# Attention on 64-row halves and half of a dense network moved behind it: an attention and expert kernel on one core

## Chip, core and metric

One NeuronCore of a Trainium2 chip runs the whole program. The metric is the device time of one execution, in microseconds; the time before is the median of three runs, 517.41 us (515.21 to 519.56). PE is the matrix engine (PEld its weight loads), DVE the vector engine, ACT the scalar engine with the activation functions, POOL the general engine that also issues the software DMA queue, SP the engine that only issues DMAs.

## The reference

```python
q_n, k_n = rmsnorm(q, g_q), rmsnorm(k, g_k)          # batch 8, 12 heads, 448 tokens, 64 wide
scores = q_n @ k_n.T / sqrt(64)
attn = exp(scores - max) ; attn /= attn.sum(-1) + 1e-9
x = (attn @ v).transpose(0, 2, 1, 3).reshape(3584, 768)
y_dense = relu(x @ w1_dense) @ w2_dense              # 768 -> 512 -> 768
expert = argmax(x @ w_gate) ; gate = its softmax weight  # 8 experts
out = y_dense + gate * (relu(x @ w1[expert]) @ w2[expert])
```

All arrays are float32; `rmsnorm(x, g)` is x divided by the root of its mean square over the 64 elements, times g. Each token goes to one expert.

## The kernel before

**Attention.** Work runs over 48 head pairs t (8 batches of 6). Two pairs share one load: q and k come as float32 through SP, v as bf16 through POOL. A head's 448 tokens lie on 112 partitions, 4 tokens each (L141, pieces of 1024 bytes). POOL squares q and k (L161), DVE sums them (L162), ACT makes the reciprocal root by Ln and Exp (L167, L168), DVE normalises both (L177). PE transposes them (L186), DVE copies the result out of PSUM, multiplying q by both gains (L191, L193). For each quarter j of the keys PE makes the scores of both heads, each on its 64 rows of the array (L202), and ACT one Exp over both, 896 elements a partition (L204). PE multiplies the exponentials with v and a column of ones (L215, four key quarters into each of four query blocks); DVE divides by that column (L219, L221). The attention output of a pair is transposed (L228) and copied by ACT (L230). After six pairs `route` makes the logits, picks the expert, and writes the bf16 rows and the gate weight to a table of records in DRAM (L260 to L264).

**Dense network.** Both dense GEMMs of the batch before (`dense1`, L273, and `dense2`, L284) are cut into pieces and laid between the attention steps. The float32 result goes into the records as well (L293). A record is 1536 bytes of x, 3072 of dense result, 256 with the gate.

**Order.** The order on PE, POOL and SP is the written one; a scheduler orders DVE and ACT. For each t the loop puts the scores of t+1, the transposes of t+2, the values of t and the dense pieces in turn; loads are issued one group (two pairs) ahead of their squares. The 16 expert weights (float32 in DRAM, cast to bf16 in flight on POOL's queue, 768 KB each in the chip) are issued every 2.5 pairs (L329).

**Slot plan and slot tiles.** After attention DVE ranks all tokens by expert at once (L360 to L442): counts by scans, one selection matrix of 128x4096 (L410), a matrix of slots (L413, L416), and 32 matmuls that put the token numbers in slot order (L422). Then 35 tiles of 128 slots follow: POOL gathers their records (L449, four tiles ahead), PE transposes x (L460), multiplies with the expert's first matrix, chosen by a register (L469), ACT applies relu and gate (L474), PE transposes (L479) and multiplies with the second (L487), DVE adds the dense result (L493), and POOL scatters the rows to the output (L495).

Of the kernel before, what the change touches and what calls it, by code (L numbers as in the profile page):

```python
# [8 lines left out]
F32 = mybir.dt.float32  # L9
BF16 = mybir.dt.bfloat16  # L10
# [7 lines left out]
def kernel(  # L18
# [21 lines left out]
    JJ = 4  # L40
    SC = S // JJ
# [4 lines left out]
    FT = F // P  # L46
    De = D + 1
    scale = 1.0 / (D ** 0.5)
    QC = (0, 128, 256, S - 128)
# [6 lines left out]
    nc.vector.memset(eps_t, 1e-6)  # L56
    gq2 = const.tile([P, 1], F32)
    gk2 = const.tile([P, 1], F32)
    for hh in range(2):
        nc.sync.dma_start(gq2[hh * D:(hh + 1) * D, :], g_q.unsqueeze(1))  # L60
        nc.sync.dma_start(gk2[hh * D:(hh + 1) * D, :], g_k.unsqueeze(1))
# [4 lines left out]
    EB = E * KD * F  # L66
    NTL = N // P + E - 1
    XH = Dm // 2
    GO = XH + Dm
    NC4 = 4 * B  # L70
    tri = const.tile([P, P], BF16)
    ones = const.tile([P, P], BF16)
    nc.vector.memset(ones, 1.0)
    nc.gpsimd.affine_select(tri, ones, pattern=[[1, P]], compare_op=ALU.is_gt, fill=0.0,
                            base=0, channel_multiplier=-1)
    iop = const.tile([P, P], BF16)
    nc.gpsimd.iota(iop, pattern=[[1, P]], base=0, channel_multiplier=0,
                   allow_small_or_imprecise_dtypes=True)
    iot = const.tile([P, NTL], F32)
    nc.gpsimd.iota(iot, pattern=[[1, NTL]], base=0, channel_multiplier=0,  # L80
                   allow_small_or_imprecise_dtypes=True)
    iom = const.tile([P, NTL], F32)
    nc.vector.tensor_scalar(iom, iot, float(P), None, op0=ALU.mult)
    prio = const.tile([P, E], F32)
    nc.gpsimd.iota(prio, pattern=[[-1, E]], base=E, channel_multiplier=0,
                   allow_small_or_imprecise_dtypes=True)
    col = const.tile([P, 4], F32)
    for mi in range(4):
        nc.gpsimd.iota(col[:, mi:mi + 1], pattern=[[0, 1]], base=QC[mi], channel_multiplier=1,
                       allow_small_or_imprecise_dtypes=True)  # L90
    cmp3 = const.tile([P, 4, JJ - 1], F32)
    for jj in range(1, JJ):
        nc.vector.tensor_scalar(cmp3[:, :, jj - 1], col, float(jj * SC), None, op0=ALU.is_ge)
    colj = const.tile([P, 4], F32)
    nc.vector.tensor_reduce(colj, cmp3, AX.X, ALU.add)
    colp = const.tile([P, 4], F32)
    nc.vector.scalar_tensor_tensor(colp, in0=colj, scalar=-float(SC), in1=col,
                                   op0=ALU.mult, op1=ALU.add)
    tok = const.tile([P, B, 4, 3], BF16)
    for b in range(B):  # L100
        nc.vector.memset(tok[:, b, :, 0], float(b + 1))
        nc.vector.tensor_copy(tok[:, b, :, 1], colj)
        nc.vector.tensor_copy(tok[:, b, :, 2], colp)
    nc.vector.memset(tok[:D, :, 3, :], 0.0)

    RC = Dm // 2 + Dm + 64
    rec = nc.dram_tensor("records", (N, RC), F32).ap()
    oh = const.tile([P, B, 4, E], BF16)
    wgb = const.tile([P, KD, E], BF16)
    wd1 = const.tile([P, KD, F], BF16)  # L110
    wd2 = const.tile([P, FT, Dm], BF16)
    we = const.tile([P, E, 2, KD * F], BF16)

# [9 lines left out]
    with tc.tile_pool(name="a_ld", bufs=3) as ld, \  # L123
         tc.tile_pool(name="a_sb", bufs=2) as sb, \
         tc.tile_pool(name="a_sc", bufs=2, space=bass.MemoryType.PSUM) as scp, \
         tc.tile_pool(name="a_wk", bufs=4, space=bass.MemoryType.PSUM) as wkp:
        gts = [sb.tile([P, 4, RC - GO], F32, name=f'gt{i}', tag=f'gt{i}', bufs=1) for i in range(2)]
        for gt in gts:
            nc.vector.memset(gt, 0.0)
        xin, ssqs, rs, xn, qkT, exs, vas, xnats, xTs, hTs, vrs = [{} for _ in range(11)]  # L130

        def load(g):
            if g * GP >= NT:
                return
            b, h0 = divmod(g * GP * 2, H)
            parts = ((0, 2), (2, 4)) if g == 0 else ((0, 2 * GP),)
            for name, src in (("q", q), ("k", k)):
                xin[name, g] = ld.tile([SC, 2 * GP, JJ * D], F32, tag="x" + name, name="x" + name)
            for a, z in parts:
                for name, src in (("q", q), ("k", k)):  # L140
                    nc.sync.dma_start(  # L141
                        xin[name, g][:, a:z],
                        src[b, h0 + a:h0 + z].rearrange("h (p j) d -> p h (j d)", j=JJ))
            vr = ld.tile([SC, 2 * GP, JJ * D], BF16, tag="vr")
            nc.gpsimd.dma_start(vr, v[b, h0:h0 + 2 * GP].rearrange("h (p j) d -> p h (j d)", j=JJ))
            vrs[g] = vr
            ssqs[g] = sb.tile([SC, 2, 2 * GP * JJ], F32, tag="ssq", name="ssq")

        def values(g):
            va = ld.tile([SC, 2 * GP, JJ, D + 2], BF16, tag="va")  # L150
            nc.vector.memset(va[:, :, :, D:], 1.0)
            nc.vector.tensor_copy(va[:, :, :, :D], vrs[g].rearrange("p h (j d) -> p h j d", d=D))
            vas[g] = va

        def squares(t, names="qk"):
            g, i = divmod(t, GP)
            for name in names:
                n = "qk".index(name)
# [37 lines left out]
        def scores(t, j):  # L196
            if j == 0:
                exs[t] = sb.tile([SC, JJ, 2, S], BF16, tag="ex", name="ex")
# [353 lines left out]
```

## Time and profile before

| | us |
|---|---|
| median of the runs | 517.41 |
| the profiled execution | 519.15 |
| its span from first to last instruction | 517.3 |
| PE busy | 399.3 |
| DVE busy | 326.6 |
| ACT busy | 274.8 |
| POOL busy | 205.3 |
| first exp | 28.1 |
| last matmul of the last routing ends | 337.7 |
| first gather | 373.9 |
| first expert matmul | 383.1 |

The busy times overlap: engines work side by side, so that shares of the span add up to more than one. What counts in a stage is the engine or transfer whose end the next step waits for. The DMA engines were busy for 73% of the span (45.4% for POOL's queue, 27.6% for SP's). PE's clock was granted at 0.92 of full speed on average.

### The profile page before, as it was taken

Reading aid. Unit: us, or ns where it says so; the run is one execution under the profiler, and the core shown is the slowest. Engines: PE = TensorE matmul, PEld = TensorE weight load, DVE = VectorE, ACT = ScalarE, POOL = GpSimd, SP = SyncE. Lnnn points to the kernel's source line nnn. Section 1 sums busy time; section 2 is a strip of 40 time slices with the busy share of each in tenths; the row PEclk is TensorE's granted clock in tenths of the full one; section 3 lists DMA queues with packets and bytes.
Section 4 is the critical chain, followed back from the end, with each engine's and each line's share of the span. In section 5 each row is a group of like instructions: output and inputs, shape, how many; then the busy total and the mean of one; then the engine's idle time right before and its main releaser. Section 6 shows DMA issues by size and latency. Waiting matters only on the chain.

```text
span 517.3 us, 10774 instructions
## 1 busy us (share of the span) xinstructions
PE 399.3 (77%) x4010; PEld 232.7 (45%) x4010; DVE 326.6 (63%) x761; ACT 274.8 (53%) x431; POOL 205.3 (40%) x223
## 2 busy tenths in 40 slices
PE   0189888769688887788977979980249889899894
PEld 0046645435344454454543545650215555556552
DVE  3796999868568779588786975427603434444442
ACT  0077887648567756767855978730003333333331
POOL 6674354453426327128136130000023555556542
PEclk9999999979888989979977999996559999999998
DMA  8999679997798599959879441251063878888860
GB/s 142 237 218 175 151 154 159 192 256 96 176 269 137 137 271 142 198 133 239 187 134 248 107 144 30 81 152 46 1 241 122 278 253 266 286 283 266 294 259 2
DMA packets 66017, 92.62 MB, mean 179 GB/s; under 512 B 8749, under 2 KB 56109, under 8 KB 65968
## 3 DMA queue, kind: packets, MB, share of 16 engines
q0 software_dynamic: 31568, 52.48, 45.4%
q1 hardware_dynamic: 34400, 39.46, 27.6%
q8 instruction: 33, 0.54, 0.4%
q14 instruction: 16, 0.13, 0.1%
HBM read 83.16 MB, written 31.20 MB: 221 GB/s over the span
## 4 chain that ended last, share of the span: by engine, by line
PE 30%; DMA 27%; DVE 20%; ACT 7%; issue 6%; POOL 6%; SPq 2%; POOLq 0%; DVEq 0%; ACTq 0%
DMA xq<-in_q_dram 9%; DMA xg<-records,row 9%; DMA xk<-in_k_dram 8%; DVE y L177 7%; PE he L469 5%; PE av L215 5%; DVE ssq L162 5%; PE ps L202 5%; PE yp L487 4%; ACT ex L204 4%; POOL sq L161 4%; PE ff L273 4%; PE ff L284 2%; DVE xa L221 2%; PE tr L186 2%
## 5 line engine op out<-in xcount | busy, mean ns | idle before, releaser
L204 ACT ACTIVATE ex<-ps 112x896 bf16<-112x896 f32 x192 | 173.8, 921 | 54.3 <-PE ps L202 52.7
L161 POOL TENSOR_TENSOR sq<-xq 112x512 f32<-112x512 f32 x48 | 52.1, 1085 | 141.8 <-DMA xq<-in_q_dram 118.8
L162 DVE TENSOR_REDUCE ssq<-sq 112x8 f32<-112x512 f32 x96 | 64.0, 672 | 42.9 <-POOL sq L161 42.9
L202 PE MATMUL ps<-y 64*112 64x448 bf16 x384 | 84.1, 435 | 2.5 <-DVE y L193 1.3
L215 PE MATMUL av<-va,ex 112*128 112x65 bf16 x1536 | 71.2, 202 | 17.7 <-DVE xa L221 16.0
L215 PEld LDWEIGHTS <-ex 112*128 112x128 bf16 x1536 | 59.3, 103 | 40.9 <-DVE xa L221 21.3
L284 PE MATMUL ff<-wd,hT 128*112 128x384 bf16 x256 | 60.4, 347 | 10.8 <-DVE xa L221 10.8
L449 POOL DMA_INDIRECT xg<-records,row x35 | 33.9, 967 | 81.1 <-DVE dest L442 70.4
L186 PE MATMUL tr<-ident,y 112*128 112x112 bf16 x384 | 39.2, 232 | 29.0 <-DVE y L177 24.2
L161 POOL TENSOR_TENSOR sq<-xk 112x512 f32<-112x512 f32 x48 | 51.3, 1070 | 19.1 <-DVE ssq L162 9.8
L495 POOL DMA_INDIRECT out_dram<-ys,dest x35 | 35.6, 1018 | 58.6 <-DVE ys L493 58.6
L474 ACT ACTIVATE hs<-he,xg 128x512 bf16<-128x512 f32 x35 | 24.0, 687 | 65.6 <-DMA xg<-records,row 36.3
L469 PE MATMUL he<-we,xT 128*128 x210 | 53.5, 393 | 3.0 <-issue 1.5
L462 DVE COPY xT<-xp 128x768 bf16<-128x768 bf16 x35 | 19.5, 557 | 57.5 <-PE xp L460 57.5
L202 PEld LDWEIGHTS <-y 64*112 64x112 bf16 x384 | 26.2, 131 | 61.6 <-issue 56.0
L273 PE MATMUL ff<-xT,wd 128*128 128x448 bf16 x192 | 52.1, 373 | 2.1 <-DVE xa L221 2.1
L487 PE MATMUL yp<-we,heT 128*128 x280 | 51.2, 326 | 0.8 <-DVE ys L493 0.8
L493 DVE TENSOR_TENSOR ys<-yp,xg 128x768 f32<-128x768 f32 x35 | 33.5, 957 | 28.0 <-PE yp L487 28.0
L481 ACT COPY heT<-hp 128x512 bf16<-128x512 bf16 x35 | 20.5, 586 | 49.1 <-PE hp L479 49.1
L186 PEld LDWEIGHTS <-y 112*128 112x128 bf16 x384 | 22.9, 104 | 51.0 <-DVE y L177 25.3
L177 DVE TENSOR_TENSOR y<-xq,r 112x512 bf16<-112x512 f32 x48 | 45.0, 937 | 0.9 <-ACT r L168 0.9
L221 DVE TENSOR_TENSOR xa<-av,inv 128x256 bf16<-128x256 f32 x96 | 40.1, 418 | 1.4
(98 smaller groups left out, 473.3 us busy)
## 6 DMA issues: line engine op xcount, KB each, us to landing
we<-in_moe_w_dram POOLq DMA_DIRECT2D x16, 768.0 KB, 8.4
records<-ys SPq DMA_DIRECT2D x32, 336.0 KB, 3.3
xq<-in_q_dram SPq DMA_DIRECT2D x23, 448.0 KB, 6.7
xk<-in_k_dram SPq DMA_DIRECT2D x23, 448.0 KB, 7.0
vr<-in_v_dram POOLq DMA_DIRECT2D x24, 224.0 KB, 5.9
records<-xa SPq DMA_DIRECT2D x8, 576.0 KB, 7.4
wd<-in_moe_w_dense_dram POOLq DMA_DIRECT2D x2, 768.0 KB, 19.4
records<-xa SPq DMA_DIRECT2D x8, 96.0 KB, 7.0
```

The source lines that it names most:

```text
L161: nc.gpsimd.tensor_mul(sq, x, x)
L162: nc.vector.tensor_reduce(ssqs[g][:, n, 2 * i * JJ:(2 * i + 2) * JJ], sq.rearrange("p h (j d) -> p (h j) d", d=D), AX.X, ALU.add)
L177: nc.vector.tensor_mul(y.rearrange("p j h d -> p h j d"), x.rearrange("p h (j d) -> p h j d", d=D), rs[g][:, n, 2 * i * JJ:(2 * i + 2) * J ...
L186: nc.tensor.transpose(ps[:, j * SC:(j + 1) * SC], xn[name, t][:, j].rearrange("p h d -> p (h d)"), ident[:SC, :SC])
L202: nc.tensor.matmul(ps[:, hh, :S], qkT["k", t][d0:d0 + D, j * SC:(j + 1) * SC], qkT["q", t][d0:d0 + D, :], start=True, stop=True)
L204: nc.scalar.activation(exs[t][:, j], ps[:, :, :S], AF.Exp, scale=scale)
L215: nc.tensor.matmul(av[:, mi], exs[t][:, j, hh, QC[mi]:QC[mi] + P], vas[t // GP][:, 2 * (t % GP) + hh, j, :De], start=(j == 0), stop=(j == ...
L221: nc.vector.tensor_mul(xnats[b][:, :, h * D:(h + 1) * D], av[:, :, :D], inv.to_broadcast([P, 4, D]))
L273: nc.tensor.matmul(ffs[0], wd1[:, kk, ff * P:(ff + 1) * P], xTs[b][:, kk], start=(kk == 0), stop=(kk == KD - 1))
L284: nc.tensor.matmul(ffs[0], hTs[b][:, ff, j * SC:(j + 1) * SC], wd2[:, ff, dd * Dm // 2:(dd + 1) * Dm // 2], start=(ff == 0), stop=(ff == F ...
L469: nc.tensor.matmul(he, xTs[t][:, kk], we[:, bass.ds(eregs[t], 1), 0, kk * F:(kk + 1) * F] .rearrange("p o f -> p (o f)"), start=(kk == 0), ...
L487: nc.tensor.matmul(yp[:, dd, :HD], heTs[t][:, ff], we[:, bass.ds(eregs[t], 1), 1, ff * Dm + dd * HD:ff * Dm + (dd + 1) * HD] .rearrange("p ...
```

## The change

**Layout.** A head's 448 tokens lie on 64 partitions, 7 tokens each; two heads are stacked on the two partition halves, and a group is four heads (two such stacks), so 24 groups take the place of 48 pairs. Every operation outside PE then works on 128 partitions and 896 elements. Scores are made for 64 keys at a time and run on four 64x64 tiles of the array; values take 64 rows each.

**Norm of k.** k is loaded as bf16 through POOL's queue and never normalised. Its reciprocal root, with the factor 1/8 inside, becomes the per-partition scale of the Exp, which now covers one head (448 elements) at a time.

**Dense.** Only the first dense GEMM stays in attention; it is made token by token row, so that relu(x w1) goes into the record as 512 bf16 values. A record is 1536 bytes of x, 1024 of this, 256 with the gate. The second dense GEMM is made in the slot tiles, into the same PSUM sums as the expert's second matrix.

**Slot plan.** `route` ranks the tokens of its batch at once, with running counts, and makes its part of the selection matrix. Each expert has at least one tile.

**Weights.** Exponentials live in the space of the last experts' weights, so the last eight weight loads (experts 4 to 7) are issued among the first eight slot tiles, and the others every 2.6 groups.

The core of the diff (`...` marks what is left out):

```diff
-        nc.sync.dma_start(gq2[hh * D:(hh + 1) * D, :], g_q.unsqueeze(1))
-        nc.sync.dma_start(gk2[hh * D:(hh + 1) * D, :], g_k.unsqueeze(1))
+        nc.scalar.dma_start(gq2[hh * D:(hh + 1) * D, :], g_q.unsqueeze(1))
+        nc.scalar.dma_start(gk2[hh * D:(hh + 1) * D, :], g_k.unsqueeze(1))
...
-    GO = XH + Dm
+    GO = XH + F // 2
+    RC = GO + 64
+    LATE, WPACE = 8, 2.6
...
-         tc.tile_pool(name="a_sc", bufs=2, space=bass.MemoryType.PSUM) as scp, \
+         tc.tile_pool(name="a_sc", bufs=4, space=bass.MemoryType.PSUM) as scp, \
          tc.tile_pool(name="a_wk", bufs=4, space=bass.MemoryType.PSUM) as wkp:
+        NX = 2 * J
+        xflat = we.rearrange("p e a f -> p (e a f)")[:, -NX * 2 * S:]
...
+            return src.rearrange("b h s d -> (b h) s d")[h0:h0 + n].rearrange(
+                "(i r) (p j) d -> (r p) i (j d)", r=2, j=J)
+                xin["q", g] = ld.tile([P, 2, J * D], F32, tag="xq", name="xq", bufs=3)
+                nc.sync.dma_start(xin["q", g], heads(q, 4 * g, 4))
+                for name, src in (("k", k), ("v", v)):
+                    nc.gpsimd.dma_start(xs[name][:, n[0]:n[1]],
+                                        heads(src, 8 * u + 2 * n[0], 2 * (n[1] - n[0])))
...
+            nc.scalar.activation(r, r, AF.Exp, scale=-0.5,
+                                 bias=lns_t if name == "k" else 0.0)
...
+            for j in ((0, 1, 2, 3), (4, 5, 6))[part]:
+                for hh in range(2):
+                    nc.tensor.transpose(ps[hh * D:(hh + 1) * D, j], x[:, hh, j * D:(j + 1) * D],
+                                        ident)
...
+            pss = [scp.tile([P, 512], F32, tag="sc", name="sc") for hh in range(2)]
             for hh in range(2):
-                d0 = hh * D
-                nc.tensor.matmul(ps[:, hh, :S], qkT["k", t][d0:d0 + D, j * SC:(j + 1) * SC],
-                                 qkT["q", t][d0:d0 + D, :], start=True, stop=True)
-            nc.scalar.activation(exs[t][:, j], ps[:, :, :S], AF.Exp, scale=scale)
+                rows = slice(hh * D, (hh + 1) * D)
+                for r in range(GP):
+                    nc.tensor.matmul(pss[hh][r * D:(r + 1) * D, :S], kT[rows, r, j],
+                                     qT[rows, r].rearrange("p j s -> p (j s)"),
+                                     start=True, stop=True)
+            for hh in range(2):
+                nc.scalar.activation(x[:, hh], pss[hh][:, :S], AF.Exp,
+                                     scale=rs["k", g][:, hh, j:j + 1])
...
+            if m == 0:
+                for r in range(GP):
+                    avs[r] = wkp.tile([P, 4, De], F32, tag="wk", name="av")
+            for j in range(J):
+                for r in range(GP):
+                    rows = slice(r * D, (r + 1) * D)
+                    nc.tensor.matmul(avs[r][:, m], exs[g, j][rows, hh, QC[m]:QC[m] + P],
+                                     va[rows, hh, j, :De], start=(j == 0), stop=(j == J - 1))
...
-            nc.scalar.copy(xTs[b][:, pr], ps)
+            nc.vector.tensor_copy(xTs[b][:, gb * GP:(gb + 1) * GP], ps)
...
             nc.vector.tensor_tensor(oh[:, b], hot, m2.to_broadcast([P, 4, E]), ALU.is_equal)
+            nc.vector.memset(oh[:D, b, 3, :], 0.0)
+            rk = wkp.tile([P, 5, E], F32, tag="wk", name="rk")
+            mm = [(rk[:, :4], tri, oh[:, b])]
+            mm += [(rk[:, i:4], ones, oh[:, b, :4 - i]) for i in range(1, 4)]
+            mm += [(rk[:, 4:], ones, oh[:, b, m:m + 1]) for m in range(4)]
...
+            nc.vector.tensor_tensor(sel[:, b], iop.unsqueeze(1).to_broadcast([P, 4, P]),
+                                    lo[:, b].unsqueeze(2).to_broadcast([P, 4, P]), ALU.is_equal)
...
+        def dense(b, m, part):
+            if part == 0:
+                ff[0] = wkp.tile([P, F], F32, tag="wk", name="ff")
+            for kk in range(2 * part, 2 * part + 2):
+                nc.tensor.matmul(ff[0], xTs[b][:, kk, QC[m]:QC[m] + P], wd1[:, kk],
+                                 start=(kk == 0), stop=(kk == KD - 1))
+            if part == 2:
+                hd = sb.tile([P, F], BF16, tag="hd", bufs=1)
+                nc.scalar.activation(hd, ff[0], AF.Relu)
+                nc.sync.dma_start(rec[r0:r0 + n, XH:GO], hd[P - n:].bitcast(F32))
...
+                for g in range(NG + 1):
+                    if g % 2 == 0:
+                        load_kv(g // 2 + 2)
+                    load_q(g + 5)
+                    while nw < len(wjobs) - LATE and (nw - 2) * WPACE <= g + 1:
+                        nc.gpsimd.dma_start(*wjobs[nw])
+                    for i in range(J):
+                            scores(g + 1, i)
+                        if g + 2 < NG and i in (1, 2, 4, 5):
+                            transposes(g + 2, "qk"[i // 3], (i - 1) % 3)
+                            for n in ((0,), (1,), (2, 3), (4,), (5,), (6,), (7,))[i]:
+                                attend(g, n // 4, n % 4)
...
+            hp = ps1.tile([P, FT, P], BF16, tag="tr")
+            for i in range(FT):
+                nc.tensor.transpose(hp[:, i], xb[:, Dm + i * P:Dm + (i + 1) * P], ident)
+            nc.vector.tensor_copy(hdTs[t], hp)
...
-            eregs[t] = nc.tensor.value_load(tei[:, t:t + 1], min_val=0, max_val=E - 1)
+            eregs[t] = nc.tensor.value_load(tei[:, t:t + 1], min_val=0, max_val=min(t, E - 1))
...
+                    nc.tensor.matmul(yp[:, dd, :HD], hdTs[t][:, i],
+                                     wd2[:, i, dd * HD:(dd + 1) * HD],
+                                     start=(i == 0), stop=False)
...
-            nc.vector.tensor_add(ys, yp[:, :, :HD],
-                                 xgs[t][:, XH:GO].rearrange("p (a d) -> p a d", a=2))
+            nc.vector.tensor_copy(ys[:, 0], yp[:, 0, :HD])
+            nc.scalar.copy(ys[:, 1], yp[:, 1, :HD])
...
+                if len(wjobs) - LATE + t < len(wjobs):
+                    nc.gpsimd.dma_start(*wjobs[len(wjobs) - LATE + t])
```

## The prediction

> **What bounds the kernel now.** I read the busy time of each engine stage by stage first, then the timeline of two undisturbed places, then the chain of waits. The stages, cut at the first exp, the last routing, the first gather and the first expert matmul (columns: window, length, busy us and instructions of each engine, granted clock, DMA share, GB/s):
>
> ```profile
> 28.00:66.00 38.00, 35.50 (x398) 21.89 (x394) 31.84 (x77) 31.58 (x45) 18.46 (x19) 1.00 0.85 172
> 66.00:330.00 264.00, 222.60 (x2564) 125.95 (x2564) 201.56 (x496) 187.46 (x296) 99.33 (x103) 0.92 0.79 168
> 338.00:374.00 36.00, 12.82 (x89) 9.09 (x86) 19.51 (x49) 4.31 (x9) 0.06 (x1) 0.71 0.23 69
> 383.00:517.00 134.00, 116.57 (x828) 67.60 (x828) 51.90 (x68) 44.54 (x70) 64.64 (x65) 0.96 0.68 230
> ```
>
> So: 28 us of start, 309.6 us of attention (28.1 to 337.7), 36.3 of dense tail and slot plan, 9.2 to the first expert matmul at 383.1, 134.2 of slot tiles. In attention no engine is full; in the slot tiles PE is busy for 87%.
>
> The timeline of attention where nothing is late, and of one slot tile (start, us, engine, line):
>
> ```profile
> 320.36 0.40 PE L202 MATMUL ps<-y 64*112 64x448 bf16 x2
> 320.69 0.37 PE L186 MATMUL tr<-ident,y 112*128 112x112 bf16 x4
> 320.90 0.39 PE L228 MATMUL tr<-ident,xa 128*128 128x128 bf16 x4
> 321.13 0.54 PE L273 MATMUL ff<-xT,wd 128*128 128x448 bf16 x2
> 321.60 0.40 PE L202 MATMUL ps<-y 64*112 64x448 bf16 x2
> 321.93 0.68 PE L215 MATMUL av<-va,ex 112*128 112x65 bf16 x16
> 322.45 0.54 PE L273 MATMUL ff<-xT,wd 128*128 128x448 bf16 x2
> 322.92 0.40 PE L202 MATMUL ps<-y 64*112 64x448 bf16 x2
> ...
> 395.20 1.46 PE L469 MATMUL he<-we,xT 128*128 x6
> 396.42 1.01 POOL L495 DMA_INDIRECT out_dram<-ys,dest  x1 [0.84 <-DVE ys L493]
> 396.49 0.50 PE L460 MATMUL xp<-ident,xg 128*128 128x128 bf16 x6
> 396.83 1.46 PE L487 MATMUL yp<-we,heT 128*128 x8
> 397.73 0.96 POOL L449 DMA_INDIRECT xg<-records,row  x1 [0.30 <-ACT hs L474]
> 398.13 0.39 PE L479 MATMUL hp<-ident,hs 128*128 128x128 bf16 x4
> 398.35 1.46 PE L469 MATMUL he<-we,xT 128*128 x6
> ```
>
> The start-to-start steps are PE's price list: a scores pair 0.33 us, four transposes 0.21, sixteen value matmuls 0.52, two 448-column matmuls 0.47 before a change of array shape. A pair of 448-column scores on two row halves takes 0.40 us, two full ones 0.54: **the halves run side by side.** Four scores lie 5.2 us apart here, so a pair of head pairs (one "group" of the new kernel) costs 10.4; all 24 took 309.6, so 12.9 each. The missing 2.5 us per group is in the chain and the waits (last column the longest):
>
> ```profile
> 126.48 8.79 DMA xq<-in_q_dram
> 209.81 7.96 DMA xq<-in_q_dram
> 267.39 8.85 DMA xk<-in_k_dram
> ```
> ```profile
> POOL sq L161 <- DMA xq<-in_q_dram: 118.8, 13, 12.1
> ```
>
> Attention is PE's order plus late q and k loads, after each of which the clock drops (mean 0.92).
>
> **Part 1, start: 28 to 21 us.** q's first load stands first on SP instead of behind four g loads (q issued at 3.3 us now); k and v go to POOL's queue. POOL's squares grow from 512 to 896 elements, 1.04 to 1.8 us, four before the first scores against eight now. First exp near 21 (bounds 18 and 27).
>
> **Part 2, attention, per group.** PE: 7 scores blocks of four 64x64 tiles, 0.33 each if the four run side by side as the two do, 2.3. 28 transposes at 0.053, with four shape changes of 0.1, 1.9. Values: 112 matmuls of 65 columns on 64 rows instead of 64 on 112 rows; if halves pair up, 56 steps of 0.033, with seven shape changes 2.5. Transposes of x 0.55. Dense: four pieces of two 512-column matmuls (0.43+0.1) 2.1; the second dense GEMM (L284, 0.16 a matmul, 1.7) is gone. Routing 0.9: the new rank matmuls stand right behind the logits in PE's order and wait for five small DVE operations of 0.19 us and a memset, about 2 us per batch, with all scores queued behind. Sum 10.3.
>
> Added to it: four PSUM buffers now hold two accumulators for half a group, a q or k transpose over two slots and a dense piece over four; the next pair of accumulators waits for two reciprocals and a multiply of the old (0.17 and 0.42 each) behind DVE's reductions. I take 0.7 twice, and 0.3 for the last exp: **12.0 per group** (bounds 10.3 with all hidden, 16 with halves one after the other at the 0.053 of a transpose).
>
> ACT hides below it: an exp of 448 elements is near L276's 0.54 us, plus a pointer operand. Ln with a bias pointer took 323 ns, the Exp after it 229, so 0.09: 14 of 0.44 (back to back) to 0.53 make 6.2 to 7.4, with norms and relu 7.6 to 8.9. Its copies of x (L230, 25.5 us) go to DVE, which sheds k's normalise (39.2 us) and L291 (17.5) and stays near 8.5. POOL has 3.6 of squares and 1.4 of issues. If that cover went, ACT's 8.9 would still be under PE's 10.3.
>
> DMA: k and v land as bf16, records shrink from 4864 to 2816 bytes, eight of 16 expert loads leave. HBM traffic of the stage falls from 79 to 59 MB, and q is issued two to three groups ahead (now one): I let the 2.5 us of lateness go. What is late next is the accumulators' release.
>
> The Trainium skill, "TensorEngine Tiling (Array Packing)", Tile-to-Partition Mapping, says that column tiling turns fast weight load off, which speaks against transposes and scores of 64 output partitions. No row here is column-tiled; weights of 112 columns took 131 ns against 103 for 128. By the rule, with loads of 64/1.2 = 53 ns ("TensorE: Matmul & The Clock Gate", LDWEIGHTS; an estimate) not hidden, 28 transposes would cost 1.5 more, 34 us in all; the sum above does without.
>
> Stage: 7 (exps of group 0) + 4x9.4 (no dense yet) + 19x12.0 + 9 (last group, routing) = 282, against 309.6.
>
> **Part 3, slot plan: 36.3 to 17.** Positions are ranked per batch, so the scans, the 4.4 us selection (L410) and the shift chain leave this place; left are route's chain (4), the first part of the plan (3.5), L413, L416, L422 (1.3, 3.7, 3.0) and 1.5 of small ones. The dense tail after the last routing falls from 15 us (L273, L284, copies and store waits up to 353) to 5, beside that chain. Gathers of 360 KB instead of 622 bring the first matmul 1 us nearer: 8.
>
> **Part 4, slot tiles: 134 to 208.** From the rows: gemm1 1.29, transposes 0.34, gemm2 1.30, hidden transposes 0.22: 3.15. Each tile gains eight matmuls (1.30) and four transposes (0.22): **4.67**. ACT and DVE copies (1.04 together, one after the other in the build) fit in the 2.1 us before the next gemm2. 35 tiles: 163, against 35x3.15 = 110 plus gather waits that the longer tile covers.
>
> The late weights do not fit. On POOL each stands behind the store and the gather of a tile: 1.5 us after gemm2's end the store, 1.3 later the gather, 1.3 later the load, 8.4 to land (same loads now):
>
> ```profile
> we<-in_moe_w_dram POOLq DMA_DIRECT2D x16, 768.0 KB, 8.4
> ```
>
> That is 12.5 us behind the gemm2 that paces it. The bound on the expert number is min(t, 7), and in the build gemm1(t) waits for w1 up to that expert, whatever tile t needs. w1 of 5 follows store 1 and is due two tiles later (9.6): 2.9 late. w1 of 6 follows store 3, due 4.9+2.9 later: 4.7. w1 of 7 follows store 5, due 0.2 later: 12.3. w2 of 7 follows store 6, due in gemm2(7), 3.4 later: 9.1. Sum **29** (22 with the gathers' 6.0 to land, 41 with w_gate's 12.4). Behind each wait stand all PE work, so the next store, so the next load. After the two long ones the clock is halved, as at 383 (gemm1 2.72 instead of 1.46): 5. With the cold first tile 4.4, loops 163, tail 6.8: 208.
>
> **Sum.** 21+282+17+8+208 = 536 against 517.3; the run took 519.15, 1.85 more than its span, so 538; the median 517.41 is 0.3% below that run: **536 us**, 3.6% slower.
>
> **Rivals.** A, faster: the accumulators' release and the shape changes hide, 10.5 per group; 19x1.5+4x1 = 32 less, 504. It decides below 11.1 per group, where gain and loss cancel. For it: halves side by side; against: one PSUM pool for five users. 0.17. B: the late loads land in time, 34 less, 502; against it 8.4 and the issue place. 0.08. C: halves or weight loads one after the other, 13.5 to 16 per group, 570 to 625. 0.15. D: loads stay late, since k, v and weights share one queue: 1 to 2 per group, 558 to 582. 0.10. Forecast, 518 to 556: 0.50. Range 500 (A at its bound, 10.3 per group) to 582 (D's end), leaving out most of C. Within about 1% a measurement cannot tell it from no change: faster by more 0.20 (A, most of B), within 0.10, slower 0.70.
>
> **What would show it.** Four scores matmuls starting within some ns; value matmuls in pairs; groups 12 us apart with PE waiting for DVE at L248; first gather near 320; tiles 4.67 apart, with four holes of 3, 5, 12 and 9 us among the first eight, ended by the weight DMA. Wrong if groups lie under 11 or over 13 apart, or the holes are absent.

## The result, and the profile after

The changed kernel takes 587.09 us (median of four runs, 584.69 to 592.3) against 518.48 for the kernel before on the same chip (four runs): a ratio of 1.134, 95% interval 1.124 to 1.144. The forecast was 536, the range 500 to 582: the direction is right, the size is not, and the time lies 5 us above the range. The profiled execution took 592.3 us, 1.7 more than its span of 590.6.

The stages of the changed kernel, cut at the first exp, the last rank matmul, the first gather and the first expert matmul (columns as before: window, length, busy us of PE, PEld, DVE, ACT and POOL, granted clock, DMA share, GB/s; the first line begins at 33.0 and leaves out the first 8 us of attention):

```profile
33.00:342.30 309.30, 235.96 (x4500) 135.52 (x4554) 218.39 (x473) 212.96 (x443) 89.48 (x66) 0.82 0.51 107
342.30:367.80 25.50, 9.61 (x55) 5.36 (x54) 11.00 (x31) 2.39 (x4) 0.00 (x0) 0.67 0.17 51
367.80:375.50 7.70, 2.47 (x20) 2.10 (x22) 1.78 (x4) 0.00 (x0) 5.79 (x6) 0.63 0.64 190
375.50:590.60 215.10, 173.13 (x1222) 105.71 (x1238) 48.87 (x101) 58.07 (x105) 70.88 (x72) 0.90 0.49 133
```

| stage | before | forecast | after |
|---|---|---|---|
| start, to the first exp | 28.1 | 21 | 25.1 |
| attention, to the end of the last routing's matmuls | 309.6 | 282 | 317.2 |
| plan, to the first gather | 36.2 | 17 | 25.5 |
| gather to the first expert matmul | 9.2 | 8 | 7.7 |
| slot tiles | 134.2 | 208 | 215.1 |

The misses add up to 54.6 us: 4.1, 35.2, 8.5, -0.3 and 7.1. Two thirds of them are in attention. There the DMA share fell from 0.79 to 0.51 and PE's busy time from 265 to 243 us (7.1 of them in the first 8 us, not in the lines above), so transfers and array work did become less, and yet the stage is longer. (60 of the 192 dense matmuls, L330, left no record here; at 0.23 us, by which the second of a pair lengthens the first, that is an estimated 14 us more than the 243.) The clock was granted at 0.82 (0.93 before).

An undisturbed stretch of attention, the timeline of PE (start, us, what):

```profile
268.13 0.38 PE L228 MATMUL sc<-y 64*64 64x448 bf16 x4
268.44 0.41 PE L206 MATMUL tr<-ident,y 128*64 128x128 bf16 x8
268.79 0.40 PE L248 MATMUL av<-va,we 64*128 64x65 bf16 x14
269.11 0.38 PE L228 MATMUL sc<-y 64*64 64x448 bf16 x4
269.43 0.36 PE L206 MATMUL tr<-ident,y 128*64 128x128 bf16 x6
269.72 0.62 PE L248 MATMUL av<-va,we 64*128 64x65 bf16 x28
```

Four scores matmuls of 448 columns take 0.38 us together and the next block starts 0.31 later; 14 value matmuls take one step of 0.32, that is 46 ns a pair; eight transposes one of 0.35. So the quarters of the array do work side by side. Five groups that hold no routing lie 9.3 to 9.7 us apart (first exp to first exp); the forecast's sum for PE, 10.3, is 9.4 without its 0.9 of routing. But eight others lie 15 to 22 us apart, so that all 24 come to 12.9 on average, which is what the kernel before had. The longest step, 267.4 to 289.8, first on PE, then on DVE, then on POOL:

```profile
270.80 0.38 PE L228 MATMUL sc<-y 64*64 64x448 bf16 x4
272.03 0.19 PE L248 MATMUL av<-va,we 64*128 64x65 bf16 x1 [0.85 <-DVE y L214]
273.58 0.39 PE L248 MATMUL av<-va,we 64*128 64x65 bf16 x13 [1.36 <-DVE xa L256]
...
274.56 0.59 PE L228 MATMUL sc<-y 64*64 64x448 bf16 x4
277.26 0.64 PE L206 MATMUL tr<-ident,xk 128*64 128x128 bf16 x8 [2.11 <-DVE xT L267]
...
286.92 0.21 PE L295 MATMUL rk<-oh,tri 128*128 128x32 bf16 x1 [5.35 <-DVE oh L288]
```
```profile
267.00 4.39 DVE L177 COPY va<-xv 128x896 bf16<-128x896 bf16 x1
271.31 0.67 DVE L214 TENSOR_SCALAR y<-tr,gqk 128x896 bf16<-128x896 bf16 x1
271.90 1.07 DVE L185 TENSOR_REDUCE ssq<-sq 128x14 f32<-128x896 f32 x1
...
275.60 1.07 DVE L185 TENSOR_REDUCE ssq<-sq 128x14 f32<-128x896 f32 x1
276.60 0.61 DVE L267 COPY xT<-xt 128x896 bf16<-128x896 bf16 x1
...
279.47 4.02 DVE L194 TENSOR_TENSOR y<-xq,r 128x896 bf16<-128x896 f32 x1
283.40 0.61 DVE L216 COPY y<-tr 128x896 bf16<-128x896 bf16 x1
283.94 0.17 DVE L277 TENSOR_REDUCE mx<-lp 128x4 f32<-128x32 f32 x1
284.04 1.07 DVE L185 TENSOR_REDUCE ssq<-sq 128x14 f32<-128x896 f32 x1
```
```profile
267.80 1.70 POOL L184 TENSOR_TENSOR sq<-xq 128x896 f32<-128x896 f32 x1
269.44 1.69 POOL L184 TENSOR_TENSOR sq<-xk 128x896 f32<-128x896 bf16 x1
...
279.20 1.69 POOL L184 TENSOR_TENSOR sq<-xq 128x896 f32<-128x896 f32 x1
280.84 1.69 POOL L184 TENSOR_TENSOR sq<-xk 128x896 f32<-128x896 bf16 x1
```

The copy of v (L177, 0.39 us elsewhere) takes 4.39, and ends 0.26 after POOL's two squares; the normalising (L194, 1.08 elsewhere) takes 4.02 beside two more. Behind them wait a copy that frees PSUM for PE (L214), the division, and the routing's first reduction (L277), between whose short operations stand sums (L185) of the last group, whose first exp comes 38 us later. PE waits each time, and from 274.56 on it works at half clock (granted 0.50 from 274.4 to 289.8): the same four scores take 0.59.

What ended last, as waits (engine, line, what it waited for; total us, times, longest). PE over the whole run, then DVE behind the last routing:

```profile
PE rk L295 <- DVE oh L288: 26.0, 8, 5.6
PE he L503 <- DMA we<-in_moe_w_dram: 21.1, 3, 13.4
...
PE av L248 <- DVE y L214: 13.6, 7, 2.9
PE yp L527 <- DMA we<-in_moe_w_dram: 9.9, 1, 9.9
PE av L248 <- DVE xa L256: 7.3, 6, 1.5
```
```profile
DVE cmp L419 <- DMA records<-hd: 10.1, 1, 10.1
```

The arrival of the late weights ends waits of 31 us in the slot tiles, and the slot plan's first operation waits 10.1 us for the stores of the last dense rows (L337, from one buffer), though it uses nothing of them: by the code, its tiles lie in the space of the attention's buffers, which are free only when the last row is stored.

### The profile page after: what moved, and what is told of

It reads as the page before. It is cut to its first block, busy times and chain, and to the rows that moved or that the text cites. A ratio compares the mean times of both kernels' runs of the same rounds, so it can differ in the third digit from the quotient of the medians.

```text
span 590.6 us, 14572 instructions
## 1 busy us (share of the span) xinstructions
PE 432.2 (73%) x5886; PEld 253.7 (43%) x5964; DVE 301.1 (51%) x651; ACT 284.9 (48%) x578; POOL 190.6 (32%) x176
## 4 chain that ended last, share of the span: by engine, by line
issue 30%; PE 30%; DVE 16%; POOL 13%; DMA 5%; ACT 5%; POOLq 0%; DVEq 0%; SPq 0%; ACTq 0%
PE av L248 8%; PE sc L228 7%; POOL xg L481 6%; PE ff L330 5%; PE tr L206 4%; ACT we L232 3%; POOL out_dram L535 3%; POOL sq L184 2%; DVE va L177 2%; PE xt L264 2%; DVE y L194 2%; DVE hot L282 2%; DVE ssq L185 2%; DMA we<-in_moe_w_dram 2%; DVE xa L256 1%
## 5 line engine op out<-in xcount | busy, mean ns | idle before, releaser
L232 ACT ACTIVATE we<-sc,r 128x448 bf16<-128x448 f32 x336 | 191.3, 638 | 68.0 <-PE sc L228 67.1
L248 PE MATMUL av<-va,we 64*128 64x65 bf16 x2688 | 84.6, 206 | 23.3 <-DVE y L214 13.6
L228 PE MATMUL sc<-y 64*64 64x448 bf16 x672 | 79.6, 443 | 7.3 <-ACT we L232 2.1
L248 PEld LDWEIGHTS <-we 64*128 64x128 bf16 x2688 | 60.3, 103 | 56.1 <-issue 31.3
L503 PE MATMUL he<-we,xT 128*128 (+1 forms) x192 | 53.4, 414 | 22.9 <-DMA we<-in_moe_w_dram 21.1
L527 PE MATMUL yp<-we,heT 128*128 (+1 forms) x280 | 52.5, 332 | 9.9 <-DMA we<-in_moe_w_dram 9.9
L330 PE MATMUL ff<-wd,xT 128*128 128x512 bf16 x132 | 50.3, 445 | 9.0 <-issue 6.7
L522 PE MATMUL yp<-wd,hdT 128*128 128x384 bf16 x280 | 52.8, 333 | 1.1 <-ACT ys L534 1.1
L170 POOL DMA_DIRECT2D xk<-in_k_dram x13 | 10.4, 802 | 131.8 <-PE tr L206 131.4
L185 DVE TENSOR_REDUCE ssq<-sq 128x14 f32<-128x896 f32 x48 | 51.0, 1075 | 3.5 <-POOL sq L184 3.5
L184 POOL TENSOR_TENSOR sq<-xk 128x896 f32<-128x896 bf16 x24 | 44.0, 1835 | 7.7 <-DVE ssq L185 4.0
L177 DVE COPY va<-xv 128x896 bf16<-128x896 bf16 x24 | 36.7, 1529 | 1.5 <-DMA xv<-in_v_dram 1.5
```

Of the source, the lines that this page charges most:

```text
L177: nc.vector.tensor_copy(vabs[g % 3][:, :, :, :D], xin["v", g].rearrange("p h (j d) -> p h j d", d=D))
L184: nc.gpsimd.tensor_mul(sq, x, x)
L185: nc.vector.tensor_reduce(ssq, sq.rearrange("p h (j d) -> p h j d", d=D), AX.X, ALU.add)
L228: nc.tensor.matmul(pss[hh][r * D:(r + 1) * D, :S], kT[rows, r, j], qT[rows, r].rearrange("p j s -> p (j s)"), start=True, stop=True)
L232: nc.scalar.activation(x[:, hh], pss[hh][:, :S], AF.Exp, scale=rs["k", g][:, hh, j:j + 1])
L248: nc.tensor.matmul(avs[r][:, m], exs[g, j][rows, hh, QC[m]:QC[m] + P], va[rows, hh, j, :De], start=(j == 0), stop=(j == J - 1))
```

## Theories

**1, the coupling:** POOL's squares hold up DVE operations, and so PE. **2, the place of the ranks:** PE waits in its own order behind the logits. **3, the queue:** loads of k and v wait on POOL for a free buffer (131 us in nine waits, at L170), and the squares behind them come late and in bunches. **4, the order:** DVE's and ACT's order comes from a scheduler that plans with its own durations; it puts work of later groups ahead of what PE waits for. Theory 4 came up only after the first two sets of runs. "Attention" below is from the first to the end of the last exp in the profiled execution: 308.0 us in the changed kernel (25.1 to 333.1). That execution took 592.3 us, 5 above the median, so that differences of a few us between such stages say little. The expectations count attention some 5 us wider (313), and call the scheduler the planner.

## Experiments on one cause at a time

**The squares on ACT.**

```diff
-            nc.gpsimd.tensor_mul(sq, x, x)
+            nc.scalar.activation(sq, x, AF.Square)
```

> Edit: the squares of q and k are made by ACT (Square, same tiles) instead of POOL; all else as in the changed kernel. Theory 1 (POOL's squares, 1.69 us each and two back to back, hold up the DVE operations that read two tiles from SBUF or copy bf16: 48 us more than their undisturbed time on DVE, behind which PE waits and its clock halves): the copy of v, L177, falls from a mean of about 1.6 us to 0.4 and the choice mask, L282, to 0.19; groups lie 10 to 10.8 us apart (ACT gains 2 x 0.9), attention falls from 313 to about 255, the total from 587 to 530. Theory 2 (PE's own order: the rank matmuls, which wait for DVE right behind the logits) leaves their wait of 26 us, the total falls by less than 15. Theory 3 (the loads of k and v on POOL's queue make the squares late) expects the same gain as theory 1 here and is told apart in the next run.

Measured: 601.47 us (598.79 to 601.84), attention 326.4. No copy is stretched any more and DVE's busy time falls from 301 to 254 us, as theory 1 expected; the time does not follow. ACT now waits in front of its exps for loads that its squares need (the waits of ACT):

```profile
ACT we L232 <- PE sc L228: 28.0, 38, 2.5
ACT sq L184 <- DMA xk<-in_k_dram: 21.6, 8, 3.8
ACT sq L184 <- DMA xq<-in_q_dram: 14.3, 8, 3.3
```

Theory 1 as the whole cause falls: 47 us less of DVE's time bought nothing here. What the relief of DVE is worth by itself this run can't say, since ACT got the work (321 us busy, 285 before the edit). One thing came out by the way: the first exp is at 17.2 instead of 25.1.

**The loads of k and v behind the squares.**

```diff
-                    if g % 2 == 0:
-                        load_kv(g // 2 + 2)
...
                             if i == 3:
                                 squares(g + 3, "k")
+                        if i == 3 and g % 2 == 0:
+                            load_kv(g // 2 + 2)
```

> Edit: on POOL's queue the loads of k and v of an even group stand behind the squares of group g+3 instead of ahead of them, so that their wait for the old buffer (131 us in nine waits) no longer holds the squares up. Theory 3 (late squares) expects attention near 255 and the total near 530. Theory 1 (what counts is that squares run while DVE copies) expects the same stretched DVE operations, moved to other places: total within 15 us of 587. Theory 2: no change.

Measured: 599.69 us (599.01 to 602.13), attention 314.9. Theory 3's gain did not come: 13 us slower, since the squares now wait for data (18.8 us for q, 25.3 for k) that was issued later. Theory 1 had named a change of under 15, so this run does not speak against it.

**The ranks one group later.**

```diff
+                        if g > NB and gb == 1 and i == 5:
+                            rank(b - 1)     # the rank matmuls and what follows them, out of route
```

> Edit: the rank matmuls of a batch, and all that follows them in the routing, stand one group (seven slots) behind the logits in PE's order; nothing else is moved. Theory 2 expects the 26 us of PE's wait for the choice mask to go and the half clock after it too: total 587 to about 545. Theory 1 expects the stretched operations to stay and only their path through the rank matmuls to go: 10 to 20 us, since the stretched copies also delay the division and so the accumulators. The last batch's ranks come after the loop as before, so slot plan and slot tiles stay.

Measured: 586.39 us (584.17 to 586.9), attention 301.8. The 26 us of PE's wait are gone, and the profiled execution has 6 us less of attention; but the medians differ by 0.7, less than their spread, so that no gain is shown. From the fifth group on, up to the last three, steps of 15 to 20 us alternate with 9.6 to 11.2: the pattern of the loads of k and v, which speaks for theory 3.

**Three buffers for k and v,** alone and with the squares on ACT:

```diff
-    with tc.tile_pool(name="a_ld", bufs=2) as ld, \
+    with tc.tile_pool(name="a_ld", bufs=3) as ld, \
```

> Edit: three buffers instead of two for the loaded k and v, nothing else. Theory 3, in its new form (bunching: the load of k and v on POOL waits up to 19 us for a free buffer, the squares of its group wait behind it, and come together with those of the next group in one long iteration): POOL's wait of 131 us at L170 goes, every iteration has one pair of squares, long and short iterations disappear except for the routing's, attention falls from 313 to about 270, the total to about 545. Theory 1 (squares beside DVE's copies cost DVE 48 us wherever they stand): the stretched operations stay, one to two per iteration, attention stays above 300 and the total above 575.

> Edit: three buffers for k and v, and the squares on ACT. Theory 1, as a part beside the bunching: no DVE operation is stretched any more, attention 15 to 40 us below that of the run with three buffers and POOL's squares, total 510 to 530. Bunching alone: the same attention as there, or a little longer, since ACT gets 1.9 us per group (8.2 to 10.1) and its order is bound to the squares' loads; total 545 to 555.

Measured: 618.38 us (615.86 to 622.52), attention 331.9; with the squares on ACT 598.14 (594.43 to 599.04) and 323.5. More buffers made it 31 us slower. POOL's wait at L170 fell from 131 to 48 us, but the same edit gave the scheduler another order, and DVE's sums now wait 40.3 us for POOL's squares, which it did for 3.5 in the changed kernel (the waits of DVE in attention):

```profile
DVE ssq L185 <- POOL sq L184: 40.3, 12, 5.5
DVE y L214 <- PE tr L206: 37.1, 16, 3.3
```

Theory 3 falls in its simple form too. But the trace shows what the relief was used for: a group's normalising now stands 41.9 us ahead of its first exp (median of groups 8 to 20), against 29.3 in the changed kernel, and POOL squares q within some 6 us of its load's issue. The engines run further ahead, up to the loads, and wait there in front of PE's work: theory 4. With three buffers, moving the squares to ACT gains 20 us, 8 of them at the start; ACT then waited 29.1 us for q's loads.

**Behind attention.** Late weights ahead of the gathers, four buffers for the dense row:

```diff
+            for job in wjobs[-LATE:-LATE + 4]:
+                nc.gpsimd.dma_start(*job)
             for t in range(4):
                 gather(t)
...
-                if len(wjobs) - LATE + t < len(wjobs):
-                    nc.gpsimd.dma_start(*wjobs[len(wjobs) - LATE + t])
+                if t < 4:
+                    nc.gpsimd.dma_start(*wjobs[len(wjobs) - 4 + t])
...
-                hd = sb.tile([P, F], BF16, tag="hd", bufs=1)
+                hd = sb.tile([P, F], BF16, tag="hd", bufs=4)
```

> Edit, behind attention only: four of the eight late weight loads are issued ahead of the first gather and the other four with tiles 0 to 3 (before: one with each of tiles 0 to 7); and the row of relu(x w1) has four buffers instead of one. If the holes between slot tiles are the place of the issues, 38.6 us of holes fall to under 6 and slot tiles from 214 to about 178; if they come from the transfers' bandwidth, at least half stays. If the store of the dense row was the 10 us between the last routing and the plan, first gather comes 8 to 10 us earlier after the last routing (30 before). Total 587 to about 542; attention as before, 313.

Measured: 551.39 us (549.6 to 552.53), 36 less. Slot tiles 177.3 against 215.1: the holes were the place of the issues, not bandwidth. The buffers gave little: the wait at the plan's start falls from 10.1 to 7.7, because the last 24 dense matmuls themselves take PE 7.0 us ahead of the last store.

**All of these together:** three buffers, late ranks, early weights, four buffers for the dense row; and the same with the squares on ACT.

> Edits together: three buffers for k and v; rank matmuls one group behind the logits; four late weight loads ahead of the first gather and four with tiles 0 to 3; four buffers for the dense row. If the three causes are separate: attention 313 to about 260 (bunching 43, routing 10 to 15), the rest 36 less as measured: total near 495, below the kernel before (518). If they overlap in attention, near 510.

> The four edits of the run before and the squares on ACT. Theory 1 beside bunching: 10 to 30 us below the run with POOL's squares, 470 to 485. Without it: the same or up to 10 us above, because ACT has 10 us of work per group of some 10.5.

Measured: 563.24 us (560.18 to 567.22), attention 325.0; and 537.69 (534.35 to 543.52). Both far above what the parts would add up to. Relief of buffers, ranks and weights does not shorten attention as long as DVE's order stays. Between the two, taking the squares off POOL is worth 26 us, some 8 of them again at the start, within the 10 to 30 that theory 1 named: the coupling has its price, but more is left.

## Experiments on the order

**The written order for DVE and ACT.** The sums and roots become functions of their own and stand three to five slots behind the squares:

```diff
-        run({PE, POOL, SP})
+        run({PE, POOL, SP, DVE, ACT})
...
                             if i == 0:
                                 squares(g + 3, "q")
-                                normalise(g + 3)
-                            if i == 3:
                                 squares(g + 3, "k")
+                            if i == 3:
+                                sums(g + 3, "q")
+                            if i == 4:
+                                roots(g + 3, "q")
+                                sums(g + 3, "k")
+                            if i == 5:
+                                normalise(g + 3)
+                                roots(g + 3, "k")
```

> Edit: DVE and ACT follow the written order like PE, POOL and SP (before: a planner orders them), and the squares' sums and roots are written apart from the squares, three to five slots behind them; nothing else. Theory 4 (the planner's order: it lets DVE and ACT take the squares' sums and norms of a group two to four groups ahead, where they wait for POOL or a load, in front of copies that PE waits for now): steps between groups fall to 10 to 11 us, attention from 313 to about 265, the total from 587 to about 540. Theory 1 (squares beside DVE's copies, in whatever order): about 290 and 565. If PE's own order and its clock are the cause: no change, 313.

> Edits: written order on DVE and ACT as above, with three buffers for k and v, the rank matmuls one group later, the late weights ahead of the first gather and four buffers for the dense row. Theory 4: attention 255 to 265, total 490 to 500, below the kernel before (518). Without it: like the same edits under the planner's order, 563.

Measured, alone: 579.02 us (577.92 to 580.0), attention 293.5: less than a third of what theory 4 expected, and near the 290 that theory 1 named. PE still waits 23.0 us at the ranks there, and POOL 97.0 for the buffers of k; which of the two takes the rest wasn't told apart. With the other four edits: 534.39 (532.86 to 537.62), attention 281.0 against 325.0 for the same edits under the scheduler, though theory 4 had named 255 to 265. The two attention windows, scheduler's order first (columns as in the table of stages):

```profile
25.50:350.50 325.00, 255.22 (x4415) 135.54 (x4410) 191.82 (x456) 219.64 (x456) 95.73 (x74) 0.81 0.54 111
32.80:313.80 281.00, 222.69 (x4354) 127.54 (x4410) 195.16 (x449) 218.86 (x453) 93.07 (x71) 0.91 0.61 123
```

DVE is busy equally long in both (191.8 and 195.2 us, 220.8 in the changed kernel), and attention is 44 us apart: what differs is when DVE and ACT do their work, not how long they take (ACT 219.6 and 218.9). The edits that did nothing before do something once the order is fixed.

**Squares pinned.** As the run before, but the squares stand one group earlier, the loads of k and v two, and the sums last in DVE's iteration, so that POOL squares while DVE works out of PSUM (the lines at the old places, which go, are left out):

```diff
-                        load_kv(g // 2 + 2)
+                        load_kv(g // 2 + 3)
...
+                        if i == 0:
+                            for name in "qk":
+                                if g + 4 < NG:
+                                    squares(g + 4, name)
+                                if g + 3 < NG:
+                                    roots(g + 3, name)
+                        if i == 4 and g + 3 < NG:
+                            normalise(g + 3)
+                        if i == 4 and g + 2 < NG:
+                            values(g + 2)
+                        if i == 6 and g + 4 < NG:
+                            sums(g + 4, "q")
+                            sums(g + 4, "k")
```

> As the run before, and the squares of a group stand one group earlier, with the sums last in DVE's iteration, so that POOL's pair of squares falls beside DVE operations that read PSUM, and the copy of v and the normalising of q stand three slots behind it. Theory 1 as a part beside theory 4: the copy of v (L177) and the normalising (L194) at their undisturbed 0.39 and 1.08 us in nearly all groups, and the total 10 to 20 us below the run before. Theory 4 alone: the same total.

Measured: 505.47 us (502.76 to 511.81), 0.971 of the kernel before (0.963 to 0.979) and 29 below the run before, more than the 10 to 20 expected. Attention 253.9; groups lie 10.0, 10.6 and 12.5 to 12.8 apart, in the same turn from the sixth group on, and a group is normalised 15.1 us ahead of its first exp. The copy of v, and attention under the pinned order (the copies' min, median and max in ns, then the window's busy times):

```profile
L178 DVE COPY va<-xv x24: 380/389/390, 16.9 to 273.6; 128x896 bf16<-128x896 bf16 x24
```
```profile
33.20:287.10 253.90, 216.32 (x4354) 125.13 (x4410) 185.27 (x449) 217.40 (x453) 92.08 (x71) 0.96 0.67 137
```

DVE has the same instructions as in the changed kernel and 36 us less busy time in attention (185 against 221), PE 19 less at a clock of 0.96. The clock by slices of a fortieth of the span, changed kernel first:

```profile
PEclk9999669778879597697599885597866999999998
```
```profile
PEclk9999979999998998999989997589999999999997
```

**What of it is the order, what the place.** Undoing one part of the pinned version at a time:

```diff
-        run({PE, POOL, SP, DVE, ACT})     # DVE and ACT ordered by the scheduler again
+        run({PE, POOL, SP})
...
-                        if i == 4 and g + 2 < NG:     # the copy of v beside the squares
+                        if i == 0 and g + 2 < NG:
                             values(g + 2)
...
-                        if g > NB and gb == 1 and i == 5:     # ranks right behind the logits again
-                            rank(b - 1)
```

> Edit to the pinned version (505 us): DVE and ACT follow the planner's order again, all else as it is. Theory 4 (the planner's order): steps of 10 to 13 become 10 to 20, total 545 to 565, less the planner's quicker start (8 us). If the pinned place of the squares on POOL and the three buffers carry the gain: 495 to 510.

> Edit to the pinned version (505 us): the copy of v stands at slot 0 of the iteration, right behind the sums that release POOL's squares, instead of at slot 4, where POOL is idle; same instructions, same number. Theory 1 (DVE's copy waits until POOL's pair of squares is through): the copy takes 3 to 3.5 us instead of 0.39 in nearly every group, the accumulators' release behind it is late, total 525 to 560. If the place beside POOL costs nothing by itself: 505, within 5.

> Edit to the pinned version (505 us): the rank matmuls stand right behind the logits again, as in the changed kernel. Theory 2: each of eight routings makes PE wait for the six small operations on DVE, 1.5 to 2.5 us and the clock after it, 15 to 25 us in all: 520 to 530. If the wait is short once DVE is not held up (1.2 us by its parts): 505 to 515.

Measured: 556.78 us (555.22 to 557.87), 514.05 (508.94 to 514.49) and 515.66 (514.04 to 518.71). Attention, with the other edits in all four:

| | squares at the old place | squares pinned |
|---|---|---|
| scheduler's order | 325.0 | 316.2 |
| written order | 281.0 | 253.9 |

The order is worth 44 to 62 us of attention, the place 9 to 27, and the place pays fully only in a written order. In whole times the order is worth 29 and 51, since the written order begins 7 to 8 us later; and the execution profiled at the top left lay 4 us above its median. The upper pair differs also in k's squares, which the written order has at slot 0 instead of 3; the lower pair differs in the order alone. "Pinned" moves more than the squares: the loads of k and v, the normalising, the sums and the roots too. Of its 27 us some 10 are DVE's time (195.2 against 185.3 us, with the normalising no longer stretched), and PE's waits for the division fell from 29.5 to 12.4; which of the moves did that wasn't told apart. The copy moved beside the squares takes 1.10 us instead of 0.39, not the 3 to 3.5 that theory 1 expected, since it starts well inside the first square and waits for that one only; attention grows by 9.2 us. One such copy, and POOL beside it:

```profile
128.65 1.10 DVE L178 COPY va<-xv 128x896 bf16<-128x896 bf16 x1
```
```profile
127.82 1.67 POOL L185 TENSOR_TENSOR sq<-xq 128x896 f32<-128x896 f32 x1 [3.86 <-DVE ssq L190]
129.46 1.82 POOL L185 TENSOR_TENSOR sq<-xk 128x896 f32<-128x896 bf16 x1
```

The ranks behind the logits cost 13 us of attention, 1.9 for each of the seven batches routed inside it. PE's wait at them is then 10.5 us, 1.4 the longest, against 26.0 and 5.6 in the changed kernel: theory 2's wait was mostly DVE's lateness.

**The start.** Ahead of the loop the scheduler's order, and the squares of groups 0 to 2 on ACT (in the kernel that ran, those of group 3 stayed on POOL):

```diff
+            with tc.manual_schedule(engines={PE, POOL, SP}):     # prologue
...
+            with tc.manual_schedule(engines=order):              # loop
```

> Edit to the pinned version (505 us): ahead of the loop DVE and ACT follow the planner's order, and the squares of groups 0 to 3 are made by ACT, which is idle there; from the loop on the written order. First exp at 17 to 19 us instead of 33.2 (17.2 in the run with all squares on ACT), attention as before: total 488 to 494. If the loads set the start: not below 500.

Measured: 496.26 us (495.64 to 500.59), 0.961 of the kernel before (0.952 to 0.971). The first exp is at 17.3 instead of 33.2, but the first three groups take 30.1 us instead of 24.6, so 16 us of start became 9 of time. This version and the pinned one are faster than both kernels.

## Why the prediction was wrong, step by step

**Start, 21.** 25.1. POOL's squares took about what was priced (1.68 each, one 2.53); beside them the normalising took 1.8 and 3.1 us instead of 1.1, and POOL waited 2.7 us for DVE's sums of group 0, which the sum did not hold. With the squares on ACT it is 17.2.

**Attention, the parts of PE's sum of 10.3 a group.** Right at full clock: 9.3 to 9.7 in groups without routing, against 9.4; 10.0, 10.6 and 12.5 to 12.8 in turn in the pinned kernel. Four tiles side by side and pairs of value matmuls are as forecast, so rival C's cause is out, though the time lies in its band (570 to 625). The Trainium skill's rule that column tiling turns fast weight load off ("TensorEngine Tiling (Array Packing)", Gotcha 2: Feature Incompatibilities) would, by the prediction's estimate, have made 28 transposes 1.5 us dearer; eight of them took a step of 0.35 us, 44 ns each, against the 53 priced from before.

**"Sum 10.3", and "I take 0.7 twice, and 0.3 for the last exp: 12.0 per group."** This is the step that failed, the largest part of the miss. The 19 groups with dense work (first exps 66.1 to 322.7) lie 13.5 us apart instead of 12.0, 29 us in all. That window and the same one of the pinned kernel (columns as in the table of stages), then what PE waited for in the first:

```profile
66.10:322.70 256.60, 192.43 (x3660) 109.71 (x3709) 185.06 (x404) 177.25 (x370) 77.16 (x57) 0.81 0.54 113
67.60:278.20 210.60, 177.23 (x3638) 103.92 (x3690) 156.17 (x389) 176.28 (x369) 72.79 (x55) 0.96 0.61 129
```
```profile
PE rk L295 <- DVE oh L288: 24.7, 7, 5.6
PE av L248 <- DVE y L214: 8.6, 5, 2.4
PE av L248 <- DVE xa L256: 7.3, 6, 1.5
PE tr L206 <- DVE xT L267: 7.2, 12, 2.1
```

Two terms were too small. The ranks' wait was priced inside the 10.3 at 2 us a batch, 14 for the seven here: it took 24.7. And the clock stands at nothing: the sum holds 2 us of pauses a group and yet prices all of PE's work at full clock. Less its waits for DVE (49.5 us in all) and ACT (5.9), PE's work takes 10.6 us a group at a granted clock of 0.81, where 9.6 was priced: 19 us. The pinned kernel, with 18.0 us of waits for DVE and a clock of 0.96, has 9.9. The 0.7 twice held as a sum: the waits outside the ranks are 24.8 us, 1.3 a group. Their place was only in part the one named, the release of the accumulators by the division (L256, 7.3); more came from the copy of q's transposes out of the same PSUM buffers (L214).

Why PE waited in such long pieces is the order, which was worth 44 and 62 us of attention in the runs above. DVE's price was read from its busy time (it "stays near 8.5"; 220.8 / 24 = 9.2 were measured) as if DVE served PE first. In the scheduler's order it serves later groups first, in the changed kernel also behind copies that POOL's squares stretch to 4 us, and long pauses of PE are followed by work at half clock. That gives 12.9 a group over all 24; the same instructions take 10.65 ((278.2 - 33.2) / 23) with the order written, the squares pinned, three buffers and late ranks, and 12.3 with the written order alone. Rival A, 10.5 in the 19 groups, was reached by no run: the pinned kernel has 11.1 there (210.6 / 19). In written order the ranks behind the logits cost PE 1.3 us a batch (10.5 / 8), less than the 2 that were priced.

**"I let the 2.5 us of lateness go."** It went: PE waits for no load in attention after the start, DMA share 0.51. Rival D is out.

**Slot plan, 17.** 25.5. The dense tail, 5 us "beside that chain", is the wrong term: it takes 10.1 us from the end of the routing's chain, and the plan does not run beside it but waits for it, by the code because its tiles lie in the space of the attention's buffers. The rest, 13.2 from the plan's first operation to the first gather, was near the sum (13.0 for these parts).

**Slot tiles, 208.** 215.1. Outside the holes the tiles lie 4.68 apart, as forecast (4.67); the holes with the slow clock after them are worth 37.8 us (215.1 less the 177.3 without them), where 29 and 5 were priced. Rival B, weights in time, was out for the changed kernel, and moving the issues makes it true.

## What to carry to other kernels

An engine that is busy for some 70% of a stage can still set its pace, if its order is not that of the engine that waits: look at what stands in front of the awaited operation on that engine, and for when it is needed. Where a scheduler sets that order, removing one wait lets it run further ahead and can cost time; fix the order first and then judge buffers, queues and places one by one. A sum that holds pauses of PE needs a term for its clock as well. Weights that are due early in a stage are issued ahead of the stage's own requests on that queue.

## What the runs showed of the hardware

**POOL's squares and DVE.** In the changed kernel 16 DVE operations behind the 40 us mark were stretched by POOL's squares, by about 40 us in all: copies from SBUF to SBUF in bf16, and operations with two inputs in SBUF, down to one of 32 elements (L282, 0.19 us, 4.48 at the most). Sums (L185) and operations out of PSUM (L214, L256) never were. The Trainium skill, "SBUF — State Buffer", Who interferes with whom, states that such a DVE operation and a POOL operation exclude each other for a whole instruction. The runs agree and go further: 10 of the 16 waited for two squares in a row. Six of those began while POOL was issuing a DMA just ahead of its squares, three within 0.03 us of the first square's start and one 0.27 after it; the six that waited for one square began 0.4 us or more into it. In the run with the copy at slot 0, 19 copies took 1.10 and one, which began 0.75 us into a square, took 2.86: when the turn passes is not settled.

**The clock.** In the step shown, pauses of 0.85 and 1.36 us within 3 us stand right ahead of half clock: the granted clock is 1.00 from 271.0 to 274.3 and 0.50 from 274.4 to 289.8. Attention ran at 0.82 in the changed kernel, 0.96 in the pinned one.
